# Windowed attention with global tokens, then a two-layer MLP: the head's GpSimd queue, the bias sum, and the order of roundings rearranged

## The chip, the cores and the metric

The kernel runs on one core of a Trainium2 chip. Its time is the device time of one execution in microseconds (us). TensorE (PE) multiplies matrices into PSUM, VectorE (DVE) and ScalarE (ACT) do the elementwise work, GpSimd (POOL) does casts, small copies and address work, and SyncE (SP) issues DMAs. Each engine runs its own instructions in order. ScalarE, SyncE and GpSimd each have a queue for the DMAs that they issue.

## The reference

There are 8 batches of 8 heads, 576 positions and 64 elements per head; 8 of the positions are global. The attention output becomes a 4608 x 512 matrix that goes through a two-layer MLP.

```python
scores = scale * np.matmul(q, k.transpose(0, 1, 3, 2))
mask = np.abs(pos[:, None] - pos[None, :]) <= 32
mask = mask | is_global[:, None] | is_global[None, :]
scores = np.where(mask, scores, -1000000000.0)
attn = np.exp(scores - np.max(scores, axis=-1, keepdims=True))
attn = attn / (np.sum(attn, axis=-1, keepdims=True) + 1e-09)
x = np.matmul(attn, v).transpose(0, 2, 1, 3).reshape(B * S, H * D)
h = x @ w_in                    # 4608 x 512 @ 512 x 2048
r = np.maximum(h, 0.0)
g = s * (r * r) + b
out = g @ w_out                 # @ 2048 x 512
```

Since `b` is one number, its part of the output is `b` times the column sum of `w_out`, one row of 512 numbers that is added to every output row.

## The kernel before

**Pairs.** The attention works on 32 pairs of heads, four to a batch: pair `p` is heads `2*(p%4)` and the next of batch `p//4`. In the padded layout of 5 chunks of 128 keys, the first 8 rows of each chunk are the global tokens and 120 are ordinary keys; `W[c]` is the window of queries that a chunk of keys meets. For each chunk `qk` (L480) multiplies keys by queries into `pss`, ScalarE takes the exponential `e`, and VectorE multiplies by a band mask into `em`. `pv` (L499) has two halves of 14 matmuls in one accumulator `po`: part 0 with the values in `vring`, part 1 with ones, for the row sums. `norm_steps` (L517) takes ln and exp of the sums on ScalarE (`ln`, `rep`), collects the global queries' parts (`gs`), and writes the normalized output, transposed, into `xt`. After a batch's fourth pair, `scatter` (L553) has GpSimd write the 8 global columns over `xt` at their positions, which are held in registers (`greg_p`, L815).

**Values.** `natv` holds the loaded values of 4 pairs, `vring` their bf16 form. A slot of `vring` is filled by a cast (`cast_v`, L215) of all of it and then a copy of the global tokens' values into its first 8 partitions (`put_v`, L419), by a DMA of SP where no engine is given. Before, pair 0 is cast by ScalarE, pairs 1 to 3 by GpSimd in a row (L354), pairs 4 to 7 by ScalarE, later ones by GpSimd, two pairs ahead.

**Keys and queries.** Pairs 0 to 7 come through `six` (L111), five slots in a layout of 6 positions per partition, loaded by GpSimd's queue (`load_kq`, L152) and turned by TensorE (`trans_a`, `trans_b`). Later pairs come through `nat`, loaded by SP's queue (`load_nat`, L160), rounded by ScalarE into `natb` (`round_nat`, L181); keys are turned by a DMA transpose (`turn_k`) and queries by TensorE (`turn_q`). The rows of `natb` above 120 are filled once (L810). The keys and queries of the global tokens come through an indirect gather into `gf` (`gather`, L287), whose row numbers `grow` VectorE computes from `gidx_p`; for the first pair they are selected by a matmul (`select_first`, L679).

**The MLP.** `moe_quanta` (L564) is a generator of small pieces of TensorE work. A tile of 512 tokens is 16 pieces of 4 matmuls into `psh` (L579), each followed by Relu on ScalarE (`r`) and a square on VectorE (`g`), and then 16 pieces of 4 matmuls that make four blocks of 128 output rows in `pso` (L594). `Q` (L620) emits them between the steps of a pair.

**The order.** It is written out by hand. `first_pair` (L709) runs pairs 0 to 4 with warming matmuls on `dummy` between the real ones, as there is no MLP work yet. `run_pair` (L638) runs the rest in 8 steps: 5 steps `qk`, then the preparation of the next pair, with MLP pieces after each step. Steps at which something extra is emitted are given by `at(step, ...)` in the main loop (L853). What is put into `later` is emitted one step on.

**The bias row.** The column sums of `w_out` come by adding up: `wpiece` (L832) loads two of 16 blocks of rows at a time over GpSimd's queue into `wst`, and VectorE adds them to `wsum`, at steps 4 and 7 of pairs 7 to 14. At pair 15 `bias` (L842) sums over partitions with a matmul by `onesf`. The 8 blocks of output rows of the first two tiles come before it; they are held in SBUF (L602), and `release` (L847) adds the bias row and stores them, at two steps of some pairs from 16 on.

```python
        if 6 <= p < 14:
            adds.extend(wpiece(p - 6))
        if p == 15:
            assert not adds
            at(2, bias)
```

**GpSimd's DMAs.** Each DMA of GpSimd's queue signals one of eight semaphores in turn; an issue waits until the earlier DMA on the same semaphore has landed. The same holds for the eight of SP's. A DMA issue that waits holds up everything behind it on its engine.

Of the kernel before, what the change touches and what calls it, by code (L numbers as in the profile page):

```python
# [66 lines left out]
def kernel(  # L67
# [147 lines left out]
    def cast_v(eng, p):  # L215
        eng(out=vring[:, p % NV], in_=natv[:, p % NV])  # L216
# [56 lines left out]
    )  # L273
    grow = [const.tile([P, 1], mybir.dt.uint32, name=f"grow{i}", tag=f"grow{i}") for i in range(4)]
    gpf = const.tile([P, 1], FP32)
    nc.vector.tensor_copy(out=gpf[:], in_=gidx_p[:].bitcast(I32)[:, 0:1])

    def rows_of(bb):
        nc.vector.scalar_tensor_tensor(
# [1 line left out]
            op0=OP.add, op1=OP.add,  # L281
        )

    rows_of(0)
    gfs = {}

    def gather(bb, ts="kq"):  # L287
# [29 lines left out]
        idx6[:], pattern=[[1, NJ]], base=0, channel_multiplier=NJ,  # L317
        allow_small_or_imprecise_dtypes=True,
    )
    gadd = [const.tile([P, WM], FP32, name=f"gadd{i}", tag=f"gadd{i}") for i in range(2)]  # L320
    for t in gadd:
        nc.gpsimd.memset(t[:], 0.0)
# [5 lines left out]
    nc.gpsimd.tensor_scalar(  # L328
        out=band[:], in0=band[:], scalar1=(float(WIN) + 0.5) ** 2, scalar2=None, op0=OP.is_le
    )  # L330
    gather(0, "kqv")
    masks = []

    def build_masks(cs):
# [6 lines left out]
            )  # L341
            masks.append(view(m[:], [0, 2], [1, W[c]]))


    load_kq(2)
    load_kq(3)
    for j in range(2):
        nc.gpsimd.dma_start(
            out=win_t[:, :, 1024 * j : 1024 * j + 1024],
            in_=w_in2[:, :, 1024 * j : 1024 * j + 1024],  # L350
        )
        if j == 0:
            load_kq(4)
    for p in (1, 2, 3):  # L354
        cast_v(nc.gpsimd.tensor_copy, p)

    def load_w_out(j):
        nc.gpsimd.dma_start(
# [205 lines left out]
    def moe_quanta():  # L564
        for t in range(NTOK // 512):
            c0 = 512 * t
            gl = []
            cols = []
            a = c0
            while a < c0 + 512:  # L570
                x0 = a % (NX * S)
                n = min(c0 + 512 - a, NX * S - x0)
                cols.append((x0, a - c0, n))
                a += n
            for f in range(16):
                psh = ps_m.tile([P, 512], FP32, tag="moe", name="psh")
                for a in range(4):
                    for j, (x0, d0, n) in enumerate(cols):
                        nc.tensor.matmul(  # L579
                            psh[:, d0 : d0 + n], win_t[:, a, f * P : f * P + P],  # L580
                            xt[:, a, x0 : x0 + n],
                            start=(a == 0 and j == 0), stop=(a == 3),
                            skip_group_check=True,
                        )
                r = mop.tile([P, 512], BF16, tag="r", name="r")
                nc.scalar.activation(r[:], psh[:], AF.Relu)  # L586
                g = gpa.tile([P, 512], BF16, tag=f"g{f}", name=f"g{f}")
                gl.append(g)
                later.append(lambda g=g, r=r: nc.vector.tensor_mul(g[:], r[:], r[:]))  # L589
                yield  # L590
            for u in range(4):
                pso = ps_m.tile([P, DM], FP32, tag="moe", name="pso")
                for f in range(16):
                    nc.tensor.matmul(  # L594
                        pso[:], gl[f][:, u * P : u * P + P], wout_t[:, f],
                        start=(f == 0), stop=(f == 15),
                    )
                    if f % 4 == 3 and f < 15:
                        yield

                def store(pso=pso, r0=c0 + u * P, t=t):
                    if t < 2:  # L602
                        osb = held.tile([P, DM], FP32, tag=f"held{len(held_rows)}", name="osbh")
                        held_rows.append((osb, r0))
                        nc.vector.tensor_scalar_mul(out=osb[:], in0=pso[:], scalar1=s_bc[:])
                        return
                    osb = mop.tile([P, DM], FP32, tag="osb", name="osb")
                    nc.vector.scalar_tensor_tensor(  # L608
                        out=osb[:], in0=pso[:], scalar=s_bc[:], in1=bias_row[:],
                        op0=OP.mult, op1=OP.add,  # L610
                    )
                    nc.sync.dma_start(out=out[r0 : r0 + P, :], in_=osb[:])

                later.append(store)
                yield
# [22 lines left out]
    def run_pair(p, nq, extra, turn):  # L638

        bi, hp = divmod(p, 4)  # L640
        if hp == 0 and p > 4:
            open_batch(bi)
        for s in range(8) if p > 4 else range(NCH, 8):
            prev, later[:] = list(later), []
            now = []
            if s < NCH:
                qk(p, s)
                if s in (1, 2):
                    step()
                if s == 4 and hp == 0 and bi > 1:  # L650
                    later.append(lambda: scatter(bi - 1))
                if s == 2 and p + 1 < NSIX:
                    cast_v(A, p + 1)
                if s == 2 and NSIX <= p + 2 < NPAIR:
                    cast_v(G, p + 2)
            elif s == 5:
                if p == 4:
                    cast_v(A, 5)
                if 4 < p < NSIX - 1:
                    trans_b(p + 1, now)  # L660
                elif turn:
                    turn_q(turn, now)
            elif s == 6 and 4 < p < NSIX - 1:
                trans_a(p + 1, now)
            for f in now + prev:
                f()
            if s == 0:
                pv(p - 1)
                pending.extend(norm_steps(p - 1))
            if s == 6 and p + 1 < NSIX:  # L670
                put_v(None, p + 1)
            for f in extra.get(s, ()):
                f()
            Q(nq[s])
# [34 lines left out]
    def first_pair(p, extra={}):  # L709


        if p % 4 == 0:
            open_batch(p // 4)
        bank = idle_bank()
        for s in range(NCH):
            prev, later[:] = list(later), []
            now = []
            if p or s > 1:
                warm(1, bank)
            qk(p, s)  # L720
            if p == 4 and s > 2 or p < 4 and s < 2:
                (trans_b, trans_a)[1 - s % 2 if p == 4 else s](p + 1, now)
            if s in (1, 2):
                if p:

                    pv(p - 1, (2 - s,))
                    if s == 1:
                        pending.extend(norm_steps(p - 1))
            elif s == 3 and p < 4:
                step()  # L730
            elif s == 4 and p == 3:
                cast_v(A, 4)
            for f in prev + now:
                f()
            for f in extra.get(s, ()):
                f()
            if s == 1:
                step()
                if p == 4:
                    step()  # L740
            if s == 0 and p == 4:
                put_v(V, 4)

    gidx_f = const.tile([P, NG], FP32)
    nc.vector.tensor_copy(out=gidx_f[:], in_=g32[:, :, 0])
    sel6 = const.tile([P, NJ, NG], BF16)
# [1 line left out]
        out=sel6[:], in0=view(idx6[:], [1, NJ], [0, NG]),  # L748
        in1=view(gidx_f[:], [0, NJ], [1, NG]), op=OP.is_equal,
    )  # L750
    warm(8)
    trans_a(0)
    flush()
    trans_b(0)
    flush()
    clear(qbufs[1][0:D, 1], LQ)
    clear(qbufs[1][D:P, 0], LQ)
    select_first()
# [35 lines left out]
        f()  # L794
    flush()
    put_v(V, 0)
    for p in (1, 2, 3):
        put_v(None, p)
    load_v(nc.gpsimd, 4)
    load_kq(5)  # L800
    for p in (1, 2, 3, 4):
        first_pair(p)
        if p == 1:
            load_v(nc.gpsimd, 5)
            load_w_out(0)
        elif p == 2:
            load_kq(6)
            load_v(nc.gpsimd, 6)
            for t in natb.values():
                nc.gpsimd.memset(t[96:P], 0.0)  # L810
            onesf = const.tile([P, P], FP32)
            nc.gpsimd.memset(onesf[:], 1.0)
        elif p == 3:
            load_w_out(1)
            greg_p = [  # L815
                nc.gpsimd.value_load(g32[:1, i, 0:1], min_val=0, max_val=S - 1)  # L816
                for i in range(NG)
            ]
    flush()
    scatter(0)  # L820
    for i in (1, 2, 3):
# [1 line left out]
    gvall = const.tile([NG, (B - 2) * H * D], BF16)  # L823
    nc.sync.dma_start(out=s_bc[:], in_=_bcast_dram(moe_s[:], P))
    nc.sync.dma_start(out=b_bc[:], in_=_bcast_dram(moe_b[:], P))
    load_w_out(2)
    load_kq(7)
    load_v(nc.gpsimd, 7)
# [24 lines left out]
    for p in range(4, NPAIR):  # L853
# [26 lines left out]
        if p >= 6 and p + 2 < NPAIR:  # L880

            todo = {0: (p + 3, p + 4), 3: (p + 2, p + 3)}.get(hp, (8,) if p == 6 else ())
            for i, j in enumerate(todo):
                if j < NPAIR:
                    at(5 - 4 * i, round_nat, "k", j)
                    at(7 - 4 * i, round_nat, "q", j)
            at(7, turn_k, p + 2)
            at(7, put_v, None, p + 2)
        if p % 8 > 4 and p + 3 < NPAIR:
# [4 lines left out]
                at(1, steps[1])  # L894
        if p >= 7 and p + 1 < NPAIR:
            turn = p + 1
        if 7 <= p < 15:
            for s in (4, 7):
                if adds:
                    at(s, adds.pop(0))  # L900
        if 6 <= p < 14:
            adds.extend(wpiece(p - 6))
        if p == 15:
            assert not adds
            at(2, bias)
        if p > 15 and hp in (0, 3) and held_rows:
            at(2, release)
            at(6, release)
        run_pair(p, nq, ex, turn)
# [43 lines left out]
```

## Time and profile before

| | us |
|---|---|
| median of 7 runs | 376.78 |
| lowest and highest | 376.22, 379.08 |
| the profiled execution | 379.12 |
| its span | 377.5 |

In that execution the engines were busy as follows.

| engine | busy us | share of the span |
|---|---|---|
| PE matmul | 347.4 | 92% |
| VectorE | 236.4 | 63% |
| ScalarE | 228.1 | 60% |
| GpSimd | 87.6 | 23% |

The profile has a page with the busy share of every engine in 40 equal slices, a table of stages (busy times in chosen stretches), a list of waits (engine and line that waited, what it waited for, total, number and longest), timelines of single engines, and the chain of waits that ended last. Busy TensorE time is modelled from the starts of pipelined matmuls. "Clock" is the share of full speed that TensorE was granted. A line number in a row is that of the listing above.

### The profile page before, as it was taken

The page shows a single profiled execution, that of the slowest core. Times are in us where ns is not written, and L with a number is a line of the kernel's source. Part 1 is how long each engine was busy: PE and PEld are TensorE (multiplying, and loading weights), DVE is VectorE, ACT ScalarE, POOL GpSimd, SP SyncE. Part 2 cuts the span into 40 slices and gives each one's busy share as a digit, 9 for nine tenths or more (in the row PEclk, how much of TensorE's full clock was granted, in tenths as well). Part 3 has the DMA queues.
Part 4 walks back from the last instruction along what each step waited for, and adds up shares of the span by engine and source line. Part 5 has one row for each costly group of instructions (what it writes and reads, how often), then busy time and mean ns, then how long its engine had stood idle before and what let it go on. Part 6 is the DMA issues. An engine that isn't in the chain of part 4 may idle for free.

```text
span 377.5 us, 7674 instructions
## 1 busy us (share of the span) xinstructions
PE 347.4 (92%) x2740; PEld 181.8 (48%) x2740; DVE 236.4 (63%) x627; ACT 228.1 (60%) x439; POOL 87.6 (23%) x166
## 2 busy tenths in 40 slices
PE   5688378887999999999999999999999999999995
PEld 2244234343455555556765555555557754444442
DVE  4868617743887798757776787667657643432421
ACT  6458528952587668756876687667747832611610
POOL 6963585201312242103300300120020001000000
PEclk9669969989899999999999999999999999999999
DMA  5999669979999697565965998777042002002002
GB/s 118 195 190 203 120 94 194 226 145 197 207 185 203 180 209 143 119 140 169 213 150 137 198 190 167 175 179 153 31 89 53 2 28 85 0 28 85 0 29 84
DMA packets 125783, 50.14 MB, mean 133 GB/s; under 512 B 113464, under 2 KB 118584, under 8 KB 125744
## 3 DMA queue, kind: packets, MB, share of 16 engines
q1 hardware_dynamic: 116848, 37.32, 47.6%
q0 software_dynamic: 8544, 12.03, 16.2%
q8 instruction: 21, 0.34, 0.4%
q10 hardware_dynamic: 352, 0.30, 0.3%
q14 instruction: 18, 0.15, 0.1%
HBM read 42.26 MB, written 9.44 MB: 137 GB/s over the span
## 4 chain that ended last, share of the span: by engine, by line
PE 77%; DMA 9%; POOL 5%; ACT 2%; issue 2%; SPq 2%; POOLq 1%; DVE 1%; ACTq 0%
PE psh L579 31%; PE pso L594 31%; PE po L508 7%; PE pss L482 5%; DMA sixk<-in_k_dram 4%; PE pst L196 2%; DMA gidx_p<-in_global_idx_dram 2%; DMA vring<-gvx 2%; DMA natk<-in_k_dram 2%; SPq L171 1%; POOLq L816 1%; POOL gf L293 1%; POOL natv L171 1%; ACT r L586 1%; POOL natbk L810 1%
## 5 line engine op out<-in xcount | busy, mean ns | idle before, releaser
L579 PE MATMUL psh<-xt,win_t 128*128 128x512 bf16 (+2 forms) x704 | 140.2, 343 | 7.6 <-POOL xt L556 7.6
L594 PE MATMUL pso<-wout_t,g 128*128 128x512 bf16 x576 | 139.0, 383 | 0.0
L586 ACT ACTIVATE r<-psh 128x512 bf16<-128x512 f32 x144 | 88.4, 615 | 62.8 <-PE psh L579 58.6
L486 ACT ACTIVATE e<-pss 128x384 bf16<-128x384 f32 (+1 forms) x160 | 76.9, 483 | 54.8 <-PE pss L482 50.8
L579 PEld LDWEIGHTS <-win_t 128*128 128x128 bf16 x704 | 64.2, 98 | 62.1 <-issue 9.7
L589 DVE TENSOR_TENSOR g<-r 128x512 bf16<-128x512 bf16 x144 | 59.5, 428 | 47.8 <-ACT r L586 46.0
L594 PEld LDWEIGHTS <-g 128*128 128x128 bf16 x576 | 55.3, 99 | 65.0 <-issue 5.6
L489 DVE TENSOR_TENSOR em<-e,mask 128x384 bf16<-128x384 bf16 (+1 forms) x160 | 61.6, 386 | 39.5 <-ACT e L486 39.5
L482 PE MATMUL pss<-qbd,kt 128*128 128x384 bf16 (+1 forms) x160 | 52.0, 325 | 6.1 <-ACT e L486 3.5
L608 DVE SCALAR_TENSOR_TENSOR osb<-pso,s_bc,bias_row 128x512 f32<-128x512 f32 x28 | 21.0, 749 | 31.8 <-PE pso L594 31.7
L216 POOL CAST vring<-natv 128x640 bf16<-128x640 f32 x27 | 24.0, 906 | 72.2 <-PE po L508 70.7
L556 POOL COPY xt<-xg 128x4 bf16 x64 | 15.1, 236 | 107.4 <-DVE xt L545 99.5
L545 DVE TENSOR_TENSOR xt<-po,rep 128x600 bf16<-128x600 f32 x32 | 25.0, 780 | 1.7 <-ACT rep L542 0.9
L539 ACT ACTIVATE ln<-po 128x640 f32<-128x640 f32 x32 | 22.5, 703 | 5.0 <-PE po L508 5.0
L482 PEld LDWEIGHTS <-kt 128*128 128x128 bf16 x160 | 15.8, 99 | 20.0 <-DVE qbd L432 2.8
L542 ACT ACTIVATE rep<-ln 128x640 f32<-128x640 f32 x32 | 24.0, 750 | 0.1
L508 PE MATMUL po<-em,vring 128*64 128x160 bf16 (+3 forms) x448 | 20.0, 226 | 3.2 <-DMA vring<-gvx 1.8
L204 DVE COPY qbd<-pst 64x600 bf16<-64x600 bf16 x48 | 22.3, 464 | 0.7 <-PE pst L196 0.4
L508 PEld LDWEIGHTS <-vring 128*64 128x64 bf16 x448 | 15.8, 111 | 13.6 <-issue 9.9
L508 PE MATMUL po<-em,onesb 128*64 128x160 bf16 (+2 forms) x448 | 19.7, 226 | 0.2 <-DVE xt L545 0.2
L182 ACT CAST natbk<-natk 120x640 bf16<-120x640 f32 x24 | 17.6, 734 | 3.7 <-DMA natk<-in_k_dram 3.7
L182 ACT CAST natbq<-natq 120x640 bf16<-120x640 f32 x24 | 17.8, 743 | 0.0
(105 smaller groups left out, 215.6 us busy)
## 6 DMA issues: line engine op xcount, KB each, us to landing
natv<-in_v_dram SPq DMA_DIRECT2D x55, 150.0 KB
out_dram<-osb SPq DMA_DIRECT2D x28, 256.0 KB
natk<-in_k_dram SPq DMA_DIRECT2D x47, 150.0 KB
natq<-in_q_dram SPq DMA_DIRECT2D x47, 150.0 KB
wst<-in_moe_w_out_dram POOLq DMA_DIRECT2D x8, 512.0 KB, 6.0
win_t<-in_moe_w_in_dram POOLq DMA_DIRECT2D x2, 1024.0 KB
wout_t<-in_moe_w_out_dram POOLq DMA_DIRECT2D x4, 512.0 KB, 7.8
out_dram<-osbh SPq DMA_DIRECT2D x8, 256.0 KB
```

The costliest lines, as they stand in the source:

```text
L182: nc.scalar.copy(out=natb[t][0:KC, p % NV].rearrange("p (c h d) -> p c h d", c=NCH, h=2), in_=nat[t][0:KC, p % NV],)
L216: eng(out=vring[:, p % NV], in_=natv[:, p % NV])
L482: nc.tensor.matmul(ps[:], ktile[p][:, P * c : P * c + P], qbufs[p % 3][:, :, LO[c] : HI[c]])
L486: nc.scalar.activation(e[:], ps[:], AF.Exp, scale=SCALE)
L489: later.append(lambda: nc.vector.tensor_mul(em[:], e[:], masks[c]))
L508: nc.tensor.matmul(po[D * hh : D * hh + D, a : a + n], onesb[:] if part else vring[:, p % NV, c, hh], emt[(p, c)][:, hh, x : x + n], start ...
L542: nc.scalar.activation(rep[:], ln[:], AF.Exp, scale=-1.0)
L545: lambda: nc.vector.tensor_tensor(out=view(xt[:, hp, x0:], [KC, NCH], [HB, 2], [1, HB]), in0=halves(po[:, 0:LQ]), in1=halves(rep[:]), op=O ...
L579: nc.tensor.matmul(psh[:, d0 : d0 + n], win_t[:, a, f * P : f * P + P], xt[:, a, x0 : x0 + n], start=(a == 0 and j == 0), stop=(a == 3), s ...
L586: nc.scalar.activation(r[:], psh[:], AF.Relu)
L589: later.append(lambda g=g, r=r: nc.vector.tensor_mul(g[:], r[:], r[:]))
L594: nc.tensor.matmul(pso[:], gl[f][:, u * P : u * P + P], wout_t[:, f], start=(f == 0), stop=(f == 15),)
```

## The change

1. The global index work of VectorE (`gidx_f`, `sel6`) comes after the first key evacuation, and the row numbers of the gather (`gpf`, `grow`) after the first query evacuation. In GpSimd's queue the gather and the loads that follow keep their order.
2. The casts of pairs 1, 2 and 3 no longer run in a row ahead of pair 4's V loads: each is issued by GpSimd after the loads of one of the first pairs, with its `put_v` by SP. Pair 4's cast moves from ScalarE to GpSimd.
3. The eight register loads of the global positions move from behind pair 3 to pair 1's place in GpSimd's queue, ahead of the cast of pair 2. The fills of `natb` become two DMAs of SP from `dummy`; `onesf` is set earlier.
4. In pairs 1 to 3 the values half of `pv` goes from step 2 to step 3.
5. `put_v` of pairs 5, 6 and 7 goes from SP's queue to VectorE; that of pair 4, on VectorE already, from step 0 to step 4.
6. In the first and last pair of a batch the two roundings change places: the nearer pair is rounded at steps 1 and 3, the farther at 5 and 7. At pair 6, pair 8 is rounded at 1 and 3.
7. Bias pieces are loaded at pairs 9 to 16 and added at 10 to 17, the bias row is made at pair 18, and 12 blocks of output rows are held, the last four in slots of `six`, which is free by then.

```diff
-    nc.vector.tensor_copy(out=gpf[:], in_=gidx_p[:].bitcast(I32)[:, 0:1])
...
-    rows_of(0)
...
-    gather(0, "kqv")
...
-    for p in (1, 2, 3):
-        cast_v(nc.gpsimd.tensor_copy, p)
...
                 def store(pso=pso, r0=c0 + u * P, t=t):
-                    if t < 2:
-                        osb = held.tile([P, DM], FP32, tag=f"held{len(held_rows)}", name="osbh")
+                    if t < 3:
+                        i = r0 // P
+                        if i < 8:
+                            osb = held.tile([P, DM], FP32, tag=f"held{i}", name="osbh")
+                        else:
+                            osb = six["kq"[i // 11]].rearrange("p n h j d -> p (n h j d)")
+                            osb = osb.bitcast(FP32)[:, DM * ((i - 8) % 3) :][:, 0:DM]
...
             if s == 6 and p + 1 < NSIX:
-                put_v(None, p + 1)
+                put_v(V, p + 1)
...
-            if s in (1, 2):
-                if p:
-                    pv(p - 1, (2 - s,))
-                    if s == 1:
-                        pending.extend(norm_steps(p - 1))
-            elif s == 3 and p < 4:
+            if p and s in (1, 2 if p == 4 else 3):
+                pv(p - 1, (int(s == 1),))
+                if s == 1:
+                    pending.extend(norm_steps(p - 1))
+            if s == 3 and p < 4:
                 step()
-            elif s == 4 and p == 3:
-                cast_v(A, 4)
...
-            if s == 0 and p == 4:
+            if s == 4 and p == 4:
                 put_v(V, 4)
...
+    warm(8)
+    trans_a(0)
+    flush()
+    trans_b(0)
     gidx_f = const.tile([P, NG], FP32)
     nc.vector.tensor_copy(out=gidx_f[:], in_=g32[:, :, 0])
...
-    warm(8)
-    trans_a(0)
     flush()
-    trans_b(0)
-    flush()
+    nc.vector.tensor_copy(out=gpf[:], in_=gidx_p[:].bitcast(I32)[:, 0:1])
+    rows_of(0)
+    gather(0, "kqv")
...
     put_v(V, 0)
-    for p in (1, 2, 3):
-        put_v(None, p)
     load_v(nc.gpsimd, 4)
     load_kq(5)
+    cast_v(G, 1)
+    put_v(None, 1)
     for p in (1, 2, 3, 4):
         first_pair(p)
         if p == 1:
             load_v(nc.gpsimd, 5)
             load_w_out(0)
-        elif p == 2:
-            load_kq(6)
-            load_v(nc.gpsimd, 6)
-            for t in natb.values():
-                nc.gpsimd.memset(t[96:P], 0.0)
-            onesf = const.tile([P, P], FP32)
-            nc.gpsimd.memset(onesf[:], 1.0)
-        elif p == 3:
-            load_w_out(1)
             greg_p = [
                 nc.gpsimd.value_load(g32[:1, i, 0:1], min_val=0, max_val=S - 1)
                 for i in range(NG)
             ]
+            cast_v(G, 2)
+            put_v(None, 2)
+        elif p == 2:
+            load_kq(6)
+            load_v(nc.gpsimd, 6)
+            cast_v(G, 3)
+            put_v(None, 3)
+        elif p == 3:
+            load_w_out(1)
+            cast_v(G, 4)
...
+    for t in natb.values():
+        nc.sync.dma_start(
+            out=view(t[96:P], [DM, NV * NCH * P // DM], [1, DM]),
+            in_=view(dummy[96:P], [0, NV * NCH * P // DM], [1, DM]),
+        )
...
-                    at(5 - 4 * i, round_nat, "k", j)
-                    at(7 - 4 * i, round_nat, "q", j)
+                    at(1 + 4 * i, round_nat, "k", j)
+                    at(3 + 4 * i, round_nat, "q", j)
...
-        if 7 <= p < 15:
+        if 10 <= p < 18:
...
-        if 6 <= p < 14:
-            adds.extend(wpiece(p - 6))
-        if p == 15:
+        if 9 <= p < 17:
+            adds.extend(wpiece(p - 9))
+        if p == 18:
             assert not adds
             at(2, bias)
-        if p > 15 and hp in (0, 3) and held_rows:
+        if p > 18 and hp in (0, 3) and held_rows:
```

More of the change, by code (lines that the diff above doesn't have):

```diff
@@ L319 @@
     )
+    onesf = const.tile([P, P], FP32)
+    nc.gpsimd.memset(onesf[:], 1.0)
     gadd = [const.tile([P, WM], FP32, name=f"gadd{i}", tag=f"gadd{i}") for i in range(2)]
@@ L342, in build_masks @@
             masks.append(view(m[:], [0, 2], [1, W[c]]))
[L345 to L353, printed above, removed]
-    for p in (1, 2, 3):
-        cast_v(nc.gpsimd.tensor_copy, p)
     def load_w_out(j):
@@ L750 @@
     )
-    warm(8)
-    trans_a(0)
     flush()
-    trans_b(0)
-    flush()
+    nc.vector.tensor_copy(out=gpf[:], in_=gidx_p[:].bitcast(I32)[:, 0:1])
+    rows_of(0)
+    gather(0, "kqv")
+    load_kq(2)
+    load_kq(3)
+    for j in range(2):
+        nc.gpsimd.dma_start(
+            out=win_t[:, :, 1024 * j : 1024 * j + 1024],
+            in_=w_in2[:, :, 1024 * j : 1024 * j + 1024],
+        )
+        if j == 0:
+            load_kq(4)
     clear(qbufs[1][0:D, 1], LQ)
@@ L825 @@
     nc.sync.dma_start(out=b_bc[:], in_=_bcast_dram(moe_b[:], P))
+    for t in natb.values():
+        nc.sync.dma_start(
+            out=view(t[96:P], [DM, NV * NCH * P // DM], [1, DM]),
+            in_=view(dummy[96:P], [0, NV * NCH * P // DM], [1, DM]),
+        )
     load_w_out(2)
```

## The prediction

> **What bounds the kernel now.** I read the page's slices first, then the stages, then who waited for whom, then the timelines of PE and POOL.
>
> ```profile
> PE   5688378887999999999999999999999999999995
> PEclk9669969989899999999999999999999999999999
> DMA  5999669979999697565965998777042002002002
> ```
>
> A slice is 9.4 us. From the eleventh slice on, TensorE is full at full clock; all that can be won lies before it, and after it the change can only lose.
>
> ```profile
> 41.00:50.00 9.00, 1.42 (x29) 0.85 (x28) 3.80 (x14) 2.38 (x5) 3.94 (x11) 0.80 0.46 68
> 62.00:79.00 17.00, 13.83 (x140) 7.28 (x138) 10.78 (x31) 11.67 (x22) 4.38 (x7) 0.95 1.13 198
> 79.00:96.00 17.00, 13.95 (x89) 6.62 (x88) 7.62 (x20) 9.20 (x18) 1.44 (x2) 0.90 0.94 180
> 96.00:136.00 40.00, 40.00 (x299) 20.55 (x298) 32.56 (x80) 28.22 (x56) 11.98 (x25) 0.98 0.98 193
> ```
>
> The first number after the length is PE's busy time, the last three are granted clock, DMA share and GB/s. PE idles 7.6 us of 41 to 50, and 3 us in each of the next two stages, where the DMAs are full. The waits name the causes:
>
> ```profile
> PE psh L579 <- POOL xt L556: 7.6, 1, 7.6
> PE pss L482 <- ACT e L486: 3.5, 2, 3.1
> PE psv L407 <- DVE gb L400: 3.1, 1, 3.1
> PE po L508 <- DMA vring<-gvx: 1.8, 1, 1.8
> ACT natbk L182 <- DMA natk<-in_k_dram: 3.7, 1, 3.7
> ```
>
> The second is the fifth passed on: ScalarE stands at a rounding whose load has not landed, with the exponentials behind it. The first is GpSimd's queue, whose timeline decides this case:
>
> ```profile
> 17.68 2.16 POOL L216 CAST vring<-natv 128x640 bf16<-128x640 f32 x3
> 26.33 1.84 POOL L171 DMA_DIRECT2D natv<-in_v_dram  x2 [3.38 <-DMA win_t<-in_moe_w_in_dram]
> 28.16 0.79 POOL L358 DMA_DIRECT2D wout_t<-in_moe_w_out_dram  x1
> 33.61 0.69 POOL L155 DMA_DIRECT2D sixk<-in_k_dram  x1 [4.67 <-PE psw L707]
> 36.97 0.92 POOL L171 DMA_DIRECT2D natv<-in_v_dram  x1 [0.56 <-DMA sixk<-in_k_dram]
> 37.93 2.23 POOL L810 MEMSET natbk<- 32x2560 bf16 x1
> 40.10 2.23 POOL L810 MEMSET natbq<- 32x2560 bf16 x1
> 47.88 2.05 POOL L556 COPY xt<-xg 128x4 bf16 x8 [4.47 <-issue]
> ```
>
> A load on this queue waits until the one eight places ahead has landed, so 26.33, 33.61 and 36.97 are landings of win_t, win_t and sixk. Behind them the fills (4.4 us) and register loads (4.5) hold back the scatter, whose data VectorE finished at 42.36.
>
> **The change part by part.**
>
> *Select and gather (before 22 us).* gidx_p reaches VectorE at 7.99, with the selection tile behind it (to 8.74). The packets of the other index tile (gidx_i) end at 6.9 by the trace's DMA records. With the key evacuation (0.77) first, selection is ready near 7.7, the selecting matmuls come 1 us earlier and pair 0 starts 1 to 2 us earlier. The gather issues near 9.0 instead of 8.63. Next,
>
> ```profile
> 17.19 2.70 DVE L400 CAST gb<-gf 128x64 bf16<-128x64 f32 x1
> ```
>
> is a cast that by size takes at most 0.21 (the 128x128 one at 15.89); it stretches exactly over the three GpSimd casts. These move away, so 2.5 us more. PE reaches pair 1 near 17.3 instead of 21.69.
>
> *Casts 1 to 4 on POOL, one a pair.* Here most of that is lost again. The queue keeps its landings. Cast 1 stands behind the issues of pair 4's V and pair 5's k and q: 21.4 to 22.2. Cast 2 stands behind pair 5's V (26.33, for win_t), wout_t (to 28.95) and the eight register loads (4.47): 33.4 to 34.2. Cast 3 follows the V load that waits for sixk (36.97): 37.9 to 38.7. Each releases SP's copy of the global rows (put_v) into the same slot, and that copy is slow: the three that SP issued between 21.23 and 23.65 had their packets at 25.4 to 28.8, 4.3 to 5.5 us after issue; the one of 43.49 ended at 47.75, 4.3. So rows 2 are complete at 38.5 to 40.0, rows 3 at 43.0 to 44.2.
>
> PE wanted rows 2 at 35.44 and, with its head start, wants them near 33, even with the V half one step later. It stops there some 6 us. Then in pair 4: V matmuls 0.6, pair 2's xt 1.3, the trace's 1.47 to the V half of pair 3: 42 to 44; rows 3 gate it to 43.3 to 44.3. From there, as before from 40.08: matmuls 0.6, gs to xt 1.67, scatter 2.1 with nothing left ahead of it: first psh at 47.6 to 48.8, 48.3 taken, against 49.98. That is **1.7 us**, not the 7.6 of the wait. Cast 4 and the wout_t issue end near 40.4 and cost nothing, since the scatter waits for xt until 46. Should they stand later than xt, each costs its 0.8.
>
> Here the Trainium skill speaks against the estimate: "DMA: Bandwidth & Descriptors" (Anatomy of one DMA) fits about 2 us of setup and completion plus bytes, for GpSimd's queue; taken for SP's copies of 10 KB too (an estimate from that page), rows 3 are there at 41, psh starts near 45.5, and this part brings 4.5. The trace has the very copy, four times, at 4.3 to 5.5; I take the trace.
>
> A second rule also speaks against the casts: "SBUF — State Buffer" (Who interferes with whom) says that the port pair of VectorE and GpSimd is a lock held for a whole instruction. The 2.70 row agrees. Four casts of 0.72 alone could so block VectorE 2.9 us. On the path that would take 2.9 from the sum; but in 33 to 44 PE waits for put_v, with VectorE empty. I take 0.
>
> *Clock.* After its idle 7.6 us PE ran the first 12 psh in 4.35, later such groups in 2.6. The new stop at pair 3 costs half clock over pair 4, the one ahead of psh shrinks to 2 or 3 us. Between 0 and 1.7 saved; I take **0.3**, nearer the row, as both stops remain.
>
> *Fills by DMA, onesf.* 4.4 + 0.2 us leave POOL (counted above). SP issues two 160 KB fills ahead of pair 8's loads, which wait for the first g anyway: near 42, covered by that wait. Without it: two issues of 0.5, and the traffic. onesf goes before gadd, under the wait for the gather.
>
> *put_v of pairs 4 to 7 on VectorE.* SP's copy for pair 6 stood behind 12 loads, issued at 70.46 and took 6.49. From the qk at 74.84 to that at 80.60 are 5.76 us; a pair earlier (64.74 to 67.27) 2.53. The VectorE copy takes 0.47, behind evacuations and under matmuls, its cast long done. **3.2 us**, half of which is half clock after the stop. If VectorE were late: 0.47 each, 1.4. SP loses four waits, so its loads flow.
>
> *Head order.* At pair 8, step 1, ScalarE waited for natk of pair 12, issued last (85.32); now 11 is rounded first, which was issued 3.2 us earlier, and 12 four steps later, where no exponential follows for 4 us. Step 3 to step 4 took 4.24 where 1.03 is usual, the rest of the pair 5.18 where 3.87 is usual: **4.5 us**. Is a load late next? MoE starts 1.7 earlier, so the loads do too; pair 8 begins near 81.5 instead of 86.5. Two of the three wst pieces that fell before these loads, 0.5 MB each, are gone (about 1.5 us of queue each by the packets), and no put_v stands in SP. natk of 11 should land near 79, needed near 84; of 12 near 87, needed by 91. At pair 6 the rounding moves from step 5 to step 1, into ScalarE's fullest stretch (busy from 65 to 75): **-0.3**.
>
> *Bias pieces, twelve held rows.* 15 wsum additions and 8 wst loads go three pairs on; the bias matmul keeps its 0.86 but sits in a psh pair: **-0.2**, with the four additions more. In 96 to 136 VectorE is 81% busy and PE never waits. The output rows of pairs 15 to 17 leave the queue, where the pieces now come. Cover gone, one addition is about 0.6 on VectorE, four are 2.4. V matmuls one step later in pairs 1 to 3: order only, **0** beyond the above; the wait for ln (0.5 in each of two pairs) may go, and gs comes later instead.
>
> Residual waits, pair 1's rows among them: **-0.1**. Sum: 1.7 + 0.3 + 3.2 + 4.5 - 0.3 - 0.2 - 0.1 = 9.1. The profiled execution took 379.12 for a span of 377.5, 2.3 above the median 376.78; I take the difference from the median: **367.7 us**.
>
> **The rivals.**
> - *Copies land fast* (20%). If put_v takes 2 us because SP's queue is otherwise empty, the waits before psh mostly go, and the clock holds: 4.5 to 6 instead of 2, sum 12 to 14, about 364. For: the 6.49 copy had loads ahead of it in its own queue. Against: the four early ones did not, and took 4.3 and more.
> - *The loads stay the bound* (15%). DMA share is 1.13 and 0.94 from 62 to 96. PE runs 9 us ahead while the loads start 1.7 earlier; then the stop at pair 8 is only shifted and 3 to 5 of its 4.5, with some of the 3.2, stay: sum 3 to 6, about 372. Against: 1.5 MB less before pair 9.
> - *Bias pieces meet a shorter lead, slower* (8%). In 96 to 136 the DMAs are 0.98 busy and PE is just fed. With the lead of loads shrunk by 7 us and pieces over pairs 9 to 16, each piece may hold a pair's k by the 1.5 us measured above: 8 pieces, 12 us, less 9.1: about 379.7. It decides once a pair's transfers need more than its 9.1 us. Against: pairs 9 to 13 carried the same pieces without a wait.
> - *No change* (5%): gains and new waits cancel, for instance casts at the 2 us of the slowest one in the trace.
>
> **How the numbers follow.** The likeliest case has 52%, and its own range is 365.3 to 370.3 (copies 4.3 to 5.5, clock 0 to 1.7, a load late by a microsecond or two). With the fast copies and most of the bound by loads: 362.5 to 373.5, leaving out under two in ten. About 0.5%, 1.9 us, is what a measurement of this kernel tells from no change. Faster 0.87 (52 + 20 + 15), same 0.05, slower 0.08.
>
> **What would show it.** Right: PE waits for put_v (DMA vring<-gvx) in pair 3 for 3 us or more; first psh at 47.5 to 49; L400's cast at 0.2; no wait near 76 and none for natk near 90; the pair after the eighth begins near 91 instead of 100.07; from there to the end nothing differs. Wrong: psh before 46 (copies fast), a natk or vring wait of over 1 us after 60, or PE below full after 96, which would point to the bias pieces.

## The result, and the profile after

| | before, us | after, us |
|---|---|---|
| median | 376.81 (61 runs) | 374.69 (24 runs) |
| lowest and highest | 373.82, 380.94 | 371.21, 375.62 |
| the profiled execution | 379.12 | 371.4 |
| its span | 377.5 | 369.7 |

The ratio of the medians is 0.9932 with an interval of 0.9915 to 0.9949: faster by 2.1 us, a little over what can be told from no change, where 9.1 were forecast. The two profiled executions differ by 7.7 us, close to the forecast, which is the first hint of what went wrong: neither was a typical execution. The one of before lay 2.3 us above its median and the one of after 3.3 below.

The page of after, two rows of the slices (a slice is now 9.2 us):

```profile
PE   7684768899999999999999999999999999999995
PEclk9998599999999999999999999999999999999999
```

The deepest dip of TensorE has moved from the fifth slice to the fourth, with half clock in the fifth, and from the ninth slice on it is full. The waits of after, those of TensorE that count:

```profile
PE po L495 <- DMA vring<-gvx: 9.1, 2, 7.5
PE psh L566 <- POOL xt L543: 3.0, 1, 3.0
PE psg L375 <- DVE em L476: 3.0, 1, 3.0
PE pss L469 <- DVE qbd L419: 2.6, 3, 1.6
```

The wait on the scatter fell from 7.6 to 3.0, the ones on the exponentials and on `gb`'s last cast are gone, and 9.1 us of waiting for the copies of SP have come instead, with 3.0 in pair 0 (L375) for `gb`'s first cast, which VectorE could start only when the gather had landed. (L495, L566 and L469 are before's L508, L579 and L482; all lines behind the edits lie about 13 lower.) Where they stand is seen in PE's timeline:

```profile
27.81 0.61 PE L495 MATMUL po<-em,vring 128*64 128x160 bf16 x14 [1.56 <-DMA vring<-gvx]
...
39.30 1.01 PE L495 MATMUL po<-em,vring 128*64 128x160 bf16 x14 [7.54 <-DMA vring<-gvx]
...
49.77 2.75 PE L566 MATMUL psh<-xt,win_t 128*128 128x512 bf16 x12 [3.04 <-POOL xt L543]
...
74.22 0.31 PE L469 MATMUL pss<-qbd,kt 128*128 128x320 bf16 x1 [1.64 <-DVE qbd L419]
```

The stop of 7.54 is the one for the rows of pair 2; the same 14 matmuls then take 1.01 instead of 0.61, so the clock has dropped. GpSimd's timeline says why the rows are late:

```profile
21.26 0.88 POOL L216 CAST vring<-natv 128x640 bf16<-128x640 f32 x1
25.71 1.84 POOL L171 DMA_DIRECT2D natv<-in_v_dram  x2 [3.57 <-DMA win_t<-in_moe_w_in_dram]
27.54 0.80 POOL L345 DMA_DIRECT2D wout_t<-in_moe_w_out_dram  x1
32.38 0.74 POOL L216 CAST vring<-natv 128x640 bf16<-128x640 f32 x1 [4.04 <-DMA win_t<-in_moe_w_in_dram]
```

The second cast starts at 32.38, behind a load issue that waits for a landing, another issue, and the eight register loads, which are not counted as busy and lie in the gap of 4.04 from 28.3. They are all of it: in the run regs_late below, without them, the cast follows the issue at once. The cast ends at 33.12, SP's copy of 10 KB has to run, and PE goes on at 39.30, 6.2 us later. The stage behind the head, in the table of stages (length, PE busy, PE weight loads, VectorE, ScalarE, GpSimd, clock, DMA share, GB/s):

```profile
74.22:91.40 17.18, 17.18 (x137) 9.03 (x137) 11.06 (x30) 11.44 (x22) 2.70 (x10) 1.00 1.00 175
91.40:136.00 44.60, 44.16 (x344) 22.54 (x343) 33.51 (x83) 31.77 (x64) 11.49 (x20) 1.00 0.91 194
```

Pairs 7 and 8 now run without a gap, and pair 9 begins at 91.40, where the prediction had it near 91.

### The profile page after: what moved, and what is told of

Same layout as the page of the kernel before. It is cut to its first block, busy times and chain, and to the rows that moved or that the text cites. A ratio compares the mean times of both kernels' runs of the same rounds, so it can differ in the third digit from the quotient of the medians.

```text
span 369.7 us, 7698 instructions
## 1 busy us (share of the span) xinstructions
PE 344.2 (93%) x2740; PEld 180.8 (49%) x2740; DVE 238.7 (65%) x634; ACT 227.0 (61%) x438; POOL 83.9 (23%) x165
## 4 chain that ended last, share of the span: by engine, by line
PE 78%; DMA 8%; POOL 5%; issue 4%; DVE 3%; ACT 1%; POOLq 0%; ACTq 0%
PE pso L581 34%; PE psh L566 29%; PE po L495 7%; PE pss L469 5%; DMA natv<-in_v_dram 4%; DMA gf<-in_q_dram,grow 2%; PE pst L196 2%; POOL gf L291 1%; DMA natk<-in_k_dram 1%; POOL xt L543 1%; POOL sixk L155 1%; POOL sixq L155 1%; POOL wout_t L345 1%; PE pst L432 1%; POOL win_t L753 0%
## 5 line engine op out<-in xcount | busy, mean ns | idle before, releaser
L566 PE MATMUL psh<-xt,win_t 128*128 128x512 bf16 (+2 forms) x704 | 138.6, 341 | 3.0 <-POOL xt L543 3.0
L581 PE MATMUL pso<-wout_t,g 128*128 128x512 bf16 x576 | 137.1, 379 | 0.0
L566 PEld LDWEIGHTS <-win_t 128*128 128x128 bf16 x704 | 63.8, 98 | 56.9 <-issue 3.6
L469 PE MATMUL pss<-qbd,kt 128*128 128x384 bf16 (+1 forms) x160 | 52.6, 329 | 2.7 <-DVE qbd L419 2.6
L601 DVE SCALAR_TENSOR_TENSOR osb<-pso,s_bc,bias_row 128x512 f32<-128x512 f32 x24 | 18.0, 749 | 28.5 <-PE pso L581 28.4
L495 PE MATMUL po<-em,vring 128*64 128x160 bf16 (+3 forms) x448 | 20.1, 227 | 9.1 <-DMA vring<-gvx 9.1
L469 PEld LDWEIGHTS <-kt 128*128 128x128 bf16 x160 | 15.9, 100 | 20.0 <-DVE qbd L419 4.6
L495 PEld LDWEIGHTS <-vring 128*64 128x64 bf16 x448 | 15.8, 112 | 19.1 <-issue 18.1
L495 PE MATMUL po<-em,onesb 128*64 128x160 bf16 (+2 forms) x448 | 19.3, 223 | 0.0
## 6 DMA issues: line engine op xcount, KB each, us to landing
win_t<-in_moe_w_in_dram POOLq DMA_DIRECT2D x2, 1024.0 KB, 14.5
```

What stands on the lines that cost most here:

```text
L469: nc.tensor.matmul(ps[:], ktile[p][:, P * c : P * c + P], qbufs[p % 3][:, :, LO[c] : HI[c]])
L495: nc.tensor.matmul(po[D * hh : D * hh + D, a : a + n], onesb[:] if part else vring[:, p % NV, c, hh], emt[(p, c)][:, hh, x : x + n], start ...
L566: nc.tensor.matmul(psh[:, d0 : d0 + n], win_t[:, a, f * P : f * P + P], xt[:, a, x0 : x0 + n], start=(a == 0 and j == 0), stop=(a == 3), s ...
L581: nc.tensor.matmul(pso[:], gl[f][:, u * P : u * P + P], wout_t[:, f], start=(f == 0), stop=(f == 15),)
```

## The experiments

Each kernel ran beside before in the same session. There were three sessions, on three chips; after itself was run again in each. A pair's start is the start of its first `qk`.

### Session 1: which part of the gain is the late part's?

**before_again** is before, unchanged.

> The kernel before, unchanged, for a second profiled execution and as a measure of scatter. Theory 1 (the stops of the first profiled execution are those of every execution): the span is near 375 and the stop of ScalarE for natk near 90 us is again 3 to 4 us, the stop for the global rows near 76 us 1.8 us. Theory 2 (the first profiled execution, 379.12 where the median is 376.8, was a bad one in just these stops): one of the two is smaller by 2 us or more. Time ratio 1.00 within 0.3% in both.

Measured: 377.24 us against 377.63, ratio 0.999 [0.9962, 1.0018]; a second profile of 375.2 us of span. Its PE timeline:

```profile
36.77 0.61 PE L508 MATMUL po<-em,vring 128*64 128x160 bf16 x14 [0.47 <-ACT ln L539]
...
49.02 0.58 PE L579 MATMUL psh<-xt,win_t 128*128 128x512 bf16 x1 [9.94 <-POOL xt L556]
...
74.93 0.61 PE L508 MATMUL po<-em,vring 128*64 128x160 bf16 x14 [0.15 <-DMA vring<-gvx]
...
92.22 0.30 PE L482 MATMUL pss<-qbd,kt 128*128 128x320 bf16 x1 [3.66 <-ACT e L486]
```

Two readings of the first profile change. The stop for pair 6's rows at 75, which was 1.8 us and half clock behind it, is 0.15 here, so it was not in every execution. The stop behind the `natk` rounding is still there, 3.66. And pair 3's rows came at 36.77 instead of 40, yet the first `psh` stayed at 49: PE only waited 9.94 for GpSimd instead of 7.6. In before the start of the MLP is set by GpSimd's queue and not by the pairs.

**after_again** is after, unchanged.

> The changed kernel, unchanged, for a second profiled execution. Its first took 371.4 where the median is 374.7. Theory 1: the profile repeats the first (first psh near 49.8, ninth pair begins near 91.4, span 370) and what differs lies after 100 us. Theory 2: a typical execution loses 3 us more ahead of 91 us: longer stops for the global rows in pairs 1 to 3, or pairs 5 to 7, or half clock in more windows. Time 374 to 375, ratio 0.993.

Measured: 372.42, 0.9864 [0.9823, 0.9905]. The stops for the rows of pairs 1 and 2 are 2.35 and 8.09 us, the first `psh` starts at 50.59 and its twelve matmuls take 4.44.

**head_only** is before with the roundings exchanged and nothing else.

```diff
-                    at(5 - 4 * i, round_nat, "k", j)
-                    at(7 - 4 * i, round_nat, "q", j)
+                    at(1 + 4 * i, round_nat, "k", j)
+                    at(3 + 4 * i, round_nat, "q", j)
```

> Only the order of the roundings in the first and last pair of a batch is changed (nearer pair first). Theory 1: the whole stop near 90 us goes, 4.5 us less, 372.3. Theory 2: in a typical execution the stop is 1 to 2 us, so 375 to 376. If the rounding at step 1 of pair 6 costs what it did in the changed kernel (pair 6 took 1.8 us longer), that is taken from either.

Measured: 373.07, 0.9883 [0.9841, 0.9925], as fast as after_again. Its profiled execution was the slowest of its six, 376.64, so its rows are read with care; a stop is left at pair 9:

```profile
96.01 0.31 PE L482 MATMUL pss<-qbd,kt 128*128 128x320 bf16 x1 [2.40 <-DVE qbd L432]
```

**late_two** adds to it the copies of pairs 5 to 7 on VectorE.

```diff
             if s == 6 and p + 1 < NSIX:
-                put_v(None, p + 1)
+                put_v(V, p + 1)
```

> Order of roundings and the rows of pairs 5 to 7 written by VectorE instead of SP's queue; the head, the fills and the bias pieces stay as before. Theory 1: 4.5 + 3.2 = 7.7 us less, 369. Theory 2: 2 to 4 less, 373 to 375; then the typical saving of the whole change lies here, and the head brings nothing.

Measured: 373.29, 0.9896 [0.9855, 0.9937]. The copies bring nothing that can be measured; the stop at pair 9 is 1.50 here, in an execution near its median. The stop of 1.84 for pair 6's rows is not in head_only either, which still has SP's copies: its pair 7 takes 8.56 us, and late_two's takes 8.56 as well. So one change of order, which the forecast had at 4.5, gives all of the gain that after_again shows, as far as medians with intervals of 0.4% can tell, and the forecast's terms of 3.2 and of 2.0 for the head are missing.

### Session 2: where is the gain of the head?

**after_third** is after again.

> The changed kernel again, as the measure for the other three, and a third profile. If the head brings nothing, the first psh is at 49.5 to 51 and pair 9 begins at 91 to 94; ratio 0.986 to 0.993.

Measured: 372.14, 0.9876 [0.9847, 0.9906]; `psh` at 48.90, stops of 1.16 and 7.26.

**tail_only** keeps before's head (casts, fills, registers) and has all of the rest: the roundings, the copies of pairs 5 to 7 and the bias pieces with twelve held blocks.

```diff
+                put_v(V, p + 1)
...
+                    at(1 + 4 * i, round_nat, "k", j)
...
-        if 7 <= p < 15:
+        if 10 <= p < 18:
...
-        if 6 <= p < 14:
-            adds.extend(wpiece(p - 6))
+        if 9 <= p < 17:
+            adds.extend(wpiece(p - 9))
...
```

> The changed kernel's later part on the old head: order of roundings, rows of pairs 5 to 7 by VectorE, bias pieces three pairs on with twelve rows held; casts, register loads, fills and gather stay as before. Theory A (the head of the change brings nothing, since the stop at the rows of pair 2 takes the place of GpSimd's queue): as fast as the changed kernel within 0.3%. Theory B (the head brings the 2 us of the prediction): 2 us slower than the changed kernel. If the pieces matter, it is faster than the version with roundings and rows alone (0.990) by the stop left at pair 8 there, 1.5 to 2.4 us.

Measured: 371.81, 0.9878 [0.9844, 0.9911], the same as after_third. The new head, as a whole, brings nothing; the forecast's 2.0 for it would stand clear of the spread of the six executions of each. GpSimd and PE of tail_only:

```profile
36.33 2.23 POOL L816 MEMSET natbk<- 32x2560 bf16 x1
...
46.18 2.04 POOL L556 COPY xt<-xg 128x4 bf16 x8 [4.38 <-issue]
```

```profile
48.27 4.24 PE L579 MATMUL psh<-xt,win_t 128*128 128x512 bf16 x12 [8.04 <-POOL xt L556]
```

With the fills and the register loads still ahead of the scatter, `psh` starts at 48.27; with both away, in after, at 48.90 to 50.59. And there is no stop at pair 8 or 9, where head_only and late_two kept one: beside late_two only the bias pieces and the held blocks differ. That the pieces had been in the way of the loads is the likely reason; no run shows it apart.

**regs_late** is after with the register loads behind the fourth cast, so that cast 2 comes earlier.

```diff
             load_w_out(0)
-            greg_p = [
...
             cast_v(G, 2)
...
             cast_v(G, 4)
+            greg_p = [
```

> The changed kernel with the eight register loads at the end of GpSimd's head queue, behind the cast of pair 4, instead of ahead of the cast of pair 2. If the copy of the rows of pair 2 is held by the 4.5 us of register loads, that cast runs near 28.3 instead of 32.4, PE stops at pair 2's rows 4 us less, and the rows of pair 3 are next (42 to 44): first psh near 48, 1 to 2 us less in all. If the order of the loads doesn't matter, psh stays at 50 and the time at the changed kernel's.

Measured: 371.79, 0.9865 [0.9834, 0.9896]. Cast 2 starts at 29.21, 3.6 us earlier than in after_third, but:

```profile
37.17 1.01 PE L495 MATMUL po<-em,vring 128*64 128x160 bf16 x14 [5.66 <-DMA vring<-gvx]
...
44.58 0.61 PE L495 MATMUL po<-em,vring 128*64 128x160 bf16 x14 [2.35 <-DMA vring<-gvx]
...
49.93 4.03 PE L566 MATMUL psh<-xt,win_t 128*128 128x512 bf16 x12 [2.27 <-POOL xt L543]
```

The stop for pair 2's rows shrinks by 1.6 us, from 7.26 to 5.66, and one of 2.35 for pair 3's comes up. Each pair's rows pass through the same cast and the same slow copy, so an earlier cast moves the stop on to the next pair.

**head_dve_puts** is after with the copies of pairs 1 to 3 on VectorE, at the same places of the program.

```diff
             cast_v(G, 2)
-            put_v(None, 2)
+            put_v(V, 2)
...
```

> The changed kernel with the rows of pairs 1, 2 and 3 also written by VectorE (0.47 us each) instead of SP's copies of 5 to 6 us. If these copies are what ate the head's gain, PE waits only for the casts (21, 32.4, 37.3): first psh near 45, time 4 to 6 us below the changed kernel. If the head is held by something else (scatter, key loads), less than 2 us.

Measured: 373.05, 0.9882 [0.9849, 0.9916]: no gain.

```profile
34.62 0.34 PE L495 MATMUL po<-em,onesb 128*64 128x160 bf16 x2 [7.24 <-DVE em L476]
...
50.77 5.28 PE L566 MATMUL psh<-xt,win_t 128*128 128x512 bf16 x12 [3.04 <-POOL xt L543]
```

The wait has kept its length and changed its name. VectorE takes its instructions in order and stood at the copy, which is emitted a whole pair ahead of its use, until cast 2 was done at 33.9; the band masks `em` that PE needed first were behind it.

### Session 3: the copy at the place where it is needed

**after_fourth** is after once more.

> The changed kernel, as the measure for the other three: 371.5 to 374.7, first psh at 49 to 50.6.

Measured: 374.81, 0.9947 [0.9921, 0.9972]; stops of 2.18 and 7.78, `psh` at 50.38. This is close to the result above (0.9932), and 2.4 to 2.7 us more than in the sessions before.

**jit_puts** has the copies of pairs 1 to 3 on VectorE, each one `qk` step ahead of the matmuls that read it.

```diff
     cast_v(G, 1)
-    put_v(None, 1)
     for p in (1, 2, 3, 4):
-        first_pair(p)
+        first_pair(p, {1 if p == 4 else 2: [lambda p=p: put_v(V, p - 1)]} if p > 1 else {})
...
-            put_v(None, 2)
...
-            put_v(None, 3)
```

> The changed kernel with the rows of pairs 1, 2 and 3 written by VectorE one step ahead of their use, so that nothing of VectorE's queue stands behind a late cast before it has to. If SP's copies of 5 to 6 us ate the head's gain: rows of 2 at 33 to 34, rows of 3 at 37 to 38, first psh at 43 to 44.5 instead of 49 to 50.6, 4 to 6 us less. If the rows only let another stop through (k of pair 5 landing near 37, the scatter behind register work), psh at 46 or later and 3 us or less. If a head that ends earlier only meets loads that land later, psh is early and the time is not: the gain goes in pairs 5 to 9.

Measured: **367.57**, 0.9747 [0.9717, 0.9777].

```profile
29.35 0.61 PE L495 MATMUL po<-em,vring 128*64 128x160 bf16 x14 [1.23 <-DVE vring L408]
34.97 0.61 PE L495 MATMUL po<-em,vring 128*64 128x160 bf16 x14 [1.66 <-DVE vring L408]
38.47 0.61 PE L495 MATMUL po<-em,vring 128*64 128x160 bf16 x14 [0.55 <-DVE vring L408]
43.83 4.44 PE L566 MATMUL psh<-xt,win_t 128*128 128x512 bf16 x12 [3.05 <-POOL xt L543]
```

The stop of 7.78 becomes 1.66, the MLP starts 6.55 us earlier than in after_fourth, and the time is 7.24 less on the same chip. Not all of this is gain over the head of before: there the first `psh` started at 48.27 (tail_only), 49.02 and 49.98, so at 43.83 it is 4.4 to 6.2 earlier. That much SP's copy had eaten.

**jit_p6** is jit_puts with the rounding of pair 8 put back to steps 5 and 7 of pair 6.

```diff
-            for i, j in enumerate(todo):
+            for i, j in enumerate(todo, int(p == 6)):
```

> As the version with late rows by VectorE, and at pair 6 the rounding of pair 8 goes back to steps 5 and 7. If the rounding at step 1 stretches pair 6 (it takes 11.2 us in the changed kernel, 10.1 in the one before), another 1 us less; if pair 6's length comes from elsewhere, nothing.

Measured: **366.91**, 0.9738 [0.971, 0.9766], the fastest kernel here.

```profile
60.61 0.31 PE L469 MATMUL pss<-qbd,kt 128*128 128x320 bf16 x1 [0.60 <-DVE qbd L419]
70.71 0.31 PE L469 MATMUL pss<-qbd,kt 128*128 128x320 bf16 x1 [0.59 <-DVE qbd L419]
```

These two rows are the starts of pairs 6 and 7, 10.10 us apart; in jit_puts they are 59.91 and 71.09, 11.18 apart. The time differs by 0.66, within the spread of both.

**after_p6** is after with that rounding alone put back.

> The changed kernel with the rounding of pair 8 at pair 6 back at steps 5 and 7, alone. Rounding theory: pair 6 takes 10.1 us again, 1 us less in all, 0.3%. Other theory (the waits move with the head's end): the same time as the changed kernel.

Measured: 372.25, 0.9886 [0.986, 0.9913], 2.6 less than after_fourth in the same session. Pair 6 takes 10.09 us (65.01 to 75.10) against 11.18 (66.48 to 77.66), so 1.1 of that is the rounding. The profile of after_p6 reached pair 6 1.5 earlier than that of after_fourth, which the edit cannot have done.

### Where the time lies

Stretches between starts of pairs, in us of one profiled execution each:

| stretch | before | before_again | after | after_again | after_fourth | jit_p6 |
|---|---|---|---|---|---|---|
| to pair 5 | 54.16 | 54.09 | 52.36 | 54.87 | 54.65 | 48.76 |
| pairs 5 and 6 | 20.68 | 20.37 | 21.86 | 21.08 | 23.01 | 21.95 |
| pair 7 | 11.69 | 8.78 | 8.16 | 8.16 | 8.16 | 8.16 |
| pair 8 | 13.54 | 14.52 | 9.02 | 9.02 | 9.02 | 9.02 |
| pair 9 to the end | 277.4 | 277.4 | 278.3 | 278.1 | 278.4 | 278.1 |
| span | 377.5 | 375.2 | 369.7 | 371.2 | 373.2 | 366.0 |

Against before_again, pair 8 gives 5.5 us in every version that has the whole change behind the head. The head gives nothing in after_again and after_fourth, pairs 5 and 6 take 0.7 to 2.6 back, and the end takes 0.7 to 1.0.

## Why the prediction was right or wrong

**"put_v of pairs 4 to 7 on VectorE ... 3.2 us": this step failed, with all of its 3.2.** The stop was read rightly in the profile shown, but one profile was taken for all. In before_again it is 0.15, in head_only it is absent with SP's copies still there, and late_two, which has this edit and head_only's, is no faster than head_only. The stop and the half clock behind it make pair 7 of the profiled execution 2.9 us longer than that of before_again (11.69 against 8.78), which more than accounts for the 2.3 by which it lay above the median. Then "I take the difference from the median" subtracted from the median a stop which a typical execution does not have. (Pair 4's copy was on VectorE already, so SP loses three, not four.)

From the profiled execution the same sum would have given 379.12 - 9.1 = 370.0, and after's profiled execution took 371.4. Stretch by stretch these two executions differ by 1.8, -1.2, 3.5, 4.5 and -0.9, where the terms were 2.0, -0.3, 3.2, 4.5 and -0.2. For the head this is luck: the first `psh` came only 0.2 earlier (49.77 against 49.98), and the other 1.6 are its twelve matmuls, 2.75 us at full clock instead of 4.35, which no other profile of after repeats.

**The head, "1.7 us" and "Clock ... 0.3": this step failed too; mechanism right, its worth wrong.** Cast 2 was forecast for 33.4 to 34.2 (32.38 to 33.12 in after), the stop for pair 2's rows for some 6 us (7.3 to 8.1), SP's copy for longer than setup plus bytes, all of which came, the cast a microsecond early. The rival of fast copies, with the 2 us that the Trainium skill ("DMA: Bandwidth & Descriptors", Anatomy of one DMA) would give by the prediction's estimate, fell with it: here the copy took 6.2 from cast to use. The first `psh` was forecast for 48.3 and came at 48.9 to 50.6. Two terms were mis-sized: the stop by 1.3 to 2.1, and the scatter, taken at 2.1, which took 2.97 or 2.98 in every run with the new head. The clock brought nothing, as the twelve `psh` matmuls took 4.44 in three of the four profiles of after. The scatter's row of after has the shortest, median and longest of its 64 copies in ns, and VectorE's timeline what ran beside the longest:

```profile
L543 POOL COPY xt<-xg x64: 200/202/907, 46.8 to 307.6; 128x4 bf16 x64
```

```profile
48.52 0.16 DVE L415 COPY kt<-gkt 128x40 bf16<-128x40 bf16 x1
48.60 0.17 DVE L419 COPY qbd<-gqd 128x80 bf16<-128x80 bf16 x1
48.68 0.47 DVE L408 COPY vring<-gvx 8x640 bf16<-8x640 bf16 x1
49.08 0.30 DVE L476 TENSOR_TENSOR em<-e,mask 128x320 bf16<-128x320 bf16 x1
```

The copy of 907 ns is the seventh of the first eight, from 48.55 to 49.46; its neighbours take 0.20. It lies over these four operations of VectorE in all nine profiles with the new head. In before and tail_only VectorE does nothing during the scatter, and each of the eight takes 0.20. The third of the four is pair 4's `put_v`, which the change moved here. The prediction took 0 for VectorE and GpSimd holding each other up, as it looked at 33 to 44 only and at VectorE as the one held; the cost of some 0.9 came after 46 and fell on GpSimd. No run moves VectorE's work away from the scatter, so this cause is read from the traces and not tested.

tail_only against after_third, 371.81 and 372.14, puts the head at zero, and jit_puts shows that it could have brought 4 to 6.

**"Select and gather": early, then lost at the gather.** Pair 0 began at 9.55 instead of 12.02, earlier than the forecast 1 to 2 us, but TensorE then stood 2.97 for the gathered keys, and pair 1 began at 18.2 to 18.7 in the four profiles of after. The forecast was 17.3 against 21.69; before_again has 17.54.

**"Head order ... 4.5 us": right.** head_only took 4.6 off, with the loss at pair 6 in it. The stretch of pair 8 went from 14.5 to 10.7 in late_two, where 1.50 of stop is left, and to 9.0 in after, where it is gone. The rival in which the loads stay the bound may be seen in that 1.50, and not in after.

**"At pair 6 the rounding moves ... into ScalarE's fullest stretch ... -0.3": sign right, size wrong.** Pair 6 takes 1.1 us more with it (11.2 against 10.1), in jit_puts against jit_p6 and in after_fourth against after_p6.

**Bias pieces "-0.2": the loss was larger, and a gain was not counted.** tail_only has no stop left at pair 9, where late_two has 1.50. From pair 9 to the end after has some 0.7 to 1.0 more than before_again, with a wait of 0.40 at pair 11 among it; tail_only has 0.3 more. The rival that ends slower, pieces that hold the loads of pairs 9 to 16, did not come: PE is busy 44.16 of 44.60 us there.

**"a cast that by size takes at most 0.21 ... so 2.5 us more": a second thing read from one execution.** `gb`'s last cast takes 0.19 in after, but before_again and tail_only, both with GpSimd's three casts in a row, have it at 0.47 and 0.20: it starts 1.2 to 1.6 us earlier there, at 15.61 and 16.04, and is done when the casts begin, at 17.34 and 17.48. In the profile where they met, the cast was stretched; before does not do so every time.

With the measured values the sum is 0 for the copies of pairs 5 to 7, 0 for the head, and 4.6 for the order with pair 6's loss in it, with little for the bias pieces. after measured 5.2 and 4.7 in the first two sessions, tail_only 5.1. In the third after measured 2.0, close to the 2.1 of the result.

**What stays open.** Two microseconds of pair 5. In all four profiles of session 3 this pair took 11.2 to 11.8 us, in the others of after 9.9. The trace shows a pause without a cause. ScalarE's row of after_fourth, and the same step in after_third:

```profile
58.13 0.49 ACT L473 ACTIVATE e<-pss 128x384 bf16<-128x384 f32 x1 [2.35 <-PE psh L566]
```

```profile
54.75 0.49 ACT L473 ACTIVATE e<-pss 128x384 bf16<-128x384 f32 x1 [0.44 <-PE pss L469]
```

The scores for this exponential were multiplied at 55.85 (0.34), and it starts at 58.13, although ScalarE's last work before it ended at 55.8. By the trace it waits for TensorE alone, and none of the trace's instruction loads lies between 47.6 and 68.8. Pair 5 makes 1.9 of the 3.6 us by which after_fourth's span exceeds after_third's. The medians of before in the three sessions (377.63, 376.88, 376.76) do not rise with it. No run here separates the chip from other causes, so it is also open why after itself gained 2.0 in one session and 4.7 to 5.2 in the others.

## What to carry over

Before a stop is counted as gain, see it in more than one execution: what rests on a transfer's landing may be there in one run and gone in the next, and the time to subtract it from is that of the same execution. When a copy between two engines holds a third up, a faster engine is half of the answer, and its place in that engine's order the other half: set against SP's copy, VectorE's of 0.47 us was worth nothing a pair ahead of its use and about 7 us one step ahead. And a wait that falls from 7.6 to 3.0 us has saved only what the start behind it has moved, here nothing.

## What the hardware showed that was not expected

- A copy of 10 KB from SBUF to SBUF by SP's queue brought its rows 6.2 us after the cast's end in after, with the DMAs at a share of 1.23 and 213 GB/s (33.00 to 39.30); VectorE's copy of the same rows takes 0.47.
- TensorE's clock changes in stretches of 3.41 us or multiples of it. In after_fourth half clock was granted from 34.12 for 10.24 us, in and behind the stop of 7.78, and again from 51.19 for 3.41, though TensorE worked without a gap there: the twelve matmuls took 4.44. What came just before differs between the executions: in the 3.41 us ahead TensorE was busy for 0.81 (0.39 in after_again, 0.38 in after_third, each with half clock behind it), and for 1.58 in after, where full clock and 2.75 followed. By these four profiles, where such a stretch begins decides 1.7 us; no run here tests it or shows where the limit lies.
- GpSimd's 128x4 copies took 0.20 us each, the first eight 2.04 in all, while VectorE was idle, and one of eight took 0.91 beside a run of VectorE's SBUF copies, 2.97 in all. In before one of 0.67 (97.61) lies over an addition to `wsum` on VectorE (97.53, 0.68).
